# Block-sparse attention and a soft mixture of experts on one core: combine tiles of one width, own PSUM banks for the last pair, a new order of all steps

## The chip, the cores and the metric

The kernel runs on one core of a Trainium2 chip. Its time is the device time of one execution in microseconds (us); three executions of the kernel before took 200.78, 201.76 and 205.98 us, median 201.76 us. All names below are those of the profile: PE is the matmul engine (TensorE), PEld its weight loads, DVE the vector engine, ACT the scalar engine, POOL the GpSimd engine, SP the engine that issues nearly all DMAs.

## What is computed

Attention over 4 batches, 8 heads, 768 positions, 64 values a head; each query sees its own 96 last positions and 8 global keys, with a bias that falls with distance. Its output, 3072 tokens of 512 values, goes through a soft mixture of 8 experts with 4 slots each:

```
scores = q @ k.T / 8 + bias(distance, head), masked;  a = softmax(scores);  x = a @ v
logits = x @ phi                                # 3072 x 32
d = softmax(logits over tokens); slots = d.T @ x            # 32 x 512
h = relu(slots[e] @ w1[e]); slot_out[e] = h @ w2[e]         # 8 experts, 512 -> 1024 -> 512
c = softmax(logits over slots);  out = c @ slot_out         # 3072 x 512
```

## The kernel before

The program is written as named steps. A table, ORDER (line 53, 795 entries), names them in the order in which they are issued; each engine executes its own instructions in that order and waits by semaphores for the others. Nothing else decides the order.

**Attention.** A unit is one batch and one pair of heads, 16 units of two heads. For each: `scores` (L560, PE, three parts), `biased` (L569, DVE, adds the bias and keeps a maximum), `max_t` and `max_r` (L576, L581), `exponential` (L585, ACT), `w_hi` (L588, ACT, half precision) and its remainder `w_lo` (L595, on POOL, as `w_lo_dve` on DVE), `v_hi` and `v_lo` (L528 to L538, the same split of v; `v_hi_act` is ACT, `v_hi_dve` DVE), `values` (L612, PE), `ev_sums`, `ev_recs`, `ev_mul` (L625 to L637, DVE, the division), `tr` (L649, PE transposes; part 0 has 480 columns, part 1 has 288), `tr_copy` or `tr_copy_dve` (L654 ACT, L658 DVE, out of PSUM), and every second unit `logits` (L679). PSUM has eight banks: two for `xx` (the `values` output), two tiles `sc[0]`, `sc[1]` of two banks each for `scores`, and two small ones `m` in turn.

**Last pair.** After the last unit the four banks of `sc` become four banks `l`, handed out in turn by `left()`. In the kernel before, the logits of the last unit and its two transposes are put into `sc[0]` and `sc[1]` by a table, LAST_BANKS: both transposes are halves of one tile, `sc[1]`. Then come the softmax over tokens, `disp` (L762) and `slots` (L857).

**Experts.** `hid` (L879) and `proj` (L907) are the two matmuls of the experts; `late` reloads the places of the first weights with the second half of the second weights. `proj(0, ...)` gives output columns 0 to 255, `proj(1, ...)` columns 256 to 511; `osc`, `spread` and `sot` bring each half to four strips of 32 partitions.

**Combine.** `comb(n, b)` (L976), for half n and batch b, has seven matmuls, one for each tile of 120 tokens, the last of which has 48 tokens (TN is 120 six times and 48 once). Tile j = 2s + k reads the strip of 32 partitions number s, so the order k = 0: s = 0, 1, 2, 3 and k = 1: s = 0, 1, 2 puts four and three matmuls on different strips. Those with s < 3 write banks `l` (each bank takes two), the one with s = 3 writes a bank `m`. `outc` (L794 DVE, L797 ACT) copies each bank `l`, `outl` the bank `m` of two batches; `out` and `outl` DMAs (L988, L991) write 240 KB and 192 KB to memory. A matmul in 32-bit floats shows as two records in the trace.

**Other steps that the change moves.** `load_qk`, `load_v`, `extra`, `piece`, `free` and `late` are DMAs on SP's queue, in order; `chk_*` (L995 to L1019) compute a flag that says whether the fast path was valid; `cmax`, `csub`, `cexp`, `csum`, `crec`, `cmul` (L932 to L948) are the softmax over slots; `warm` (L549) is a matmul of a constant that is thrown away.

Of the kernel before, what the change touches and what calls it, by code (L numbers as in the profile page):

```python
# [10 lines left out]
F32 = mybir.dt.float32  # L11
# [10 lines left out]
B, H, S, D = 4, 8, 768, 64  # L22
DM = H * D
NG = 8
KB = 120
P = 128
# [19 lines left out]
OUT_PART = ((0, HF), (HF, HF))  # L46
# [266 lines left out]
def tile_attention_moe(ctx: ExitStack, tc: tile.TileContext, qk, v, phi, w1, w2, nn, out):  # L313
# [182 lines left out]
    nc.gpsimd.memset(eps[:, NJ - 1:NJ], 1.0e30)  # L496
    nc.gpsimd.memset(eps[0:TN[6], NJ - 1:NJ], RS_EPS)
    nc.scalar.activation(out=state[0:1, 4:5], in_=nc.const_aps.tensor(1.0, [1, 1], F32), func=AF.Exp)


    sc = [pss.tile([P, 2, 512], F32, name=f"sc{k}", tag=f"sc{k}") for k in range(2)]
    xx = psx.tile([P, 2, 512], F32, name="x", tag="x")
    mxs, nbs, rcs, ms = {}, {}, {}, {}

    def tb(u):
        return tbuf[u % 3]

    LAST_BANKS = {("logits", last): (0, 0), ("tr", last, 0): (1, 0), ("tr", last, 1): (1, 1)}

    def bank(key):  # L510
        if key in LAST_BANKS:
            k, i = LAST_BANKS[key]
            return sc[k][:, i]
        return psm.tile([P, 512], F32, name="m", tag="m")

    end = {}

    def left():

        if not end:  # L520
# [167 lines left out]
    def logits_all(u):  # L688
        b, p = units[u]
        if p != NP - 1:  # L690
            return
        lp = ms.pop(u)
        al = wk.tile([P, 6], F32, name="al", tag="al")
        als[b] = al
        for r, n in PARTS:
            nc.vector.tensor_tensor_reduce(out=lsb[r, 0:n], in0=lp[r, 0:n], in1=lsb[r, 0:n], scale=1.0, scalar=-3.0e38,  # L696
                                           op0=ALU.add, op1=ALU.max, accum_out=al[r, 4:5])
# [161 lines left out]
    def put(g):  # L859
        moe.put_slots(sl, mo.pop(("s", g))[:, 2 * NS * g:2 * NS * g + 2 * NS], 2 * g, 2 * g + 2)  # L860


    slv = Moe.slot_view(sl)
    parts = range(len(OUT_PART))
    hss = [xn01[:, WP:WP + DF], places[9][:, 0:DF]]
    hts = [[x.rearrange("p (c s m) -> p c s m", c=4, s=4) for x in y]
           for y in ((sacc, xn01[:, WP + DF:WP + DF + 512]), (places[10][:, 3 * DM:4 * DM], places[11][:, 3 * DM:4 * DM]))]
    osb = [places[8][:, at:at + w] for at, w in OUT_PART]
    sots = [places[8][:, DM + at:DM + at + w] for at, w in OUT_PART]
    obs = {k: places[10 + i // 3][:, DM * (i % 3):DM * (i % 3) + DM] for i, k in enumerate(OUT_SETS)}  # L870
    obl = [(places[8][:, DF:2 * DF], places[9][:, DF:2 * DF])[at // HF][:, B * (at % HF):B * (at % HF) + B * w].rearrange("p (b f) -> p b f", f=w) if at % HF + w <= HF
           else places[18][:, 0:B * w].rearrange("p (b f) -> p b f", f=w) for at, w in OUT_PART]

    def hid(a, c):
        if c == 0:
            mo["h", a] = [left(), left()]
        for n in range(2):
            for s in range(4):
                nc.tensor.matmul(out=mo["h", a][n][32 * s:32 * s + 32, :], lhsT=slv(a, c, s),  # L879
                                 rhs=wt[0, 4 * a + s, c // 2][:, (c % 2) * DF + 512 * n:(c % 2) * DF + 512 * n + 512],  # L880
                                 start=(c == 0), stop=(c == 3), skip_group_check=True)

    def relu(a, n):
        nc.scalar.activation(out=hss[a][:, 512 * n:512 * n + 512], in_=mo["h", a][n], func=AF.Relu)
# [70 lines left out]
    def by_slot(b):  # L955
        return lnat_all[:, 8 * b:8 * b + 8, :].rearrange("p t s -> p (t s)")[:, 0:2 * KB]
# [4 lines left out]
    def comb(n, b):  # L961
        w = OUT_PART[n][1]
        step = HF // w
        if w == P or b % 2 == 0:
            mo["l", n, b] = bank(("last", n, b))
        for s in range(3):
            mo["y", n, b, s] = left()
        for i in range(step):
            for k in range(2):
                for s in range(4):  # L970
                    j = 2 * s + k
                    if j == NJ:
                        continue
                    at = w * (2 * i + k) if s < 3 else w * ((b + i) % 2)
                    o = mo["y", n, b, s] if s < 3 else mo["l", n, b if w == P else b - b % 2]
                    nc.tensor.matmul(out=o[0:TN[j], at:at + w], lhsT=by_slot(b + i)[32 * s:32 * s + 32, KB * k:KB * k + TN[j]],  # L976
                                     rhs=sots[n][32 * s:32 * s + 32], start=True, stop=True)
# [117 lines left out]
def general(ctx, tc, moe, qk, v, phis, w1, w2, ngl, nlo, ident, out):  # L1095
# [113 lines left out]
    with ExitStack() as g3:  # L1209
        sb = g3.enter_context(tc.tile_pool(name="gsb3", bufs=1))  # L1210
        wp = g3.enter_context(tc.tile_pool(name="gwp", bufs=8))
        ps = g3.enter_context(tc.tile_pool(name="gps3", bufs=4, space=PSUM))
        cache = {}

        def weight(m, e, half):
            if (m, e, half) not in cache:
                t = wp.tile([P, 2048], F32, name="gw", tag="gw")
                nc.sync.dma_start(out=t, in_=(w1, w2)[m][e][:, 2048 * half:2048 * half + 2048])
                cache[(m, e, half)] = t
            return cache[(m, e, half)]  # L1220

        slv = Moe.slot_view(sl)
        hs = sb.tile([P, DF], F32, name="ghs")
        hts = [sb.tile([P, 8, P], F32, name=f"ght{a}") for a in range(2)]
        for a in range(2):
            moe.hidden(ps, slv, lambda e, half: weight(0, e, half), a, hs)
            moe.hidden_t(ps, hs, hts[a])
        moe.constants()
        st = sb.tile([P, NQ, 4], F32, name="gcs")
        ex = sb.tile([P, NQ, NS], F32, name="gex")  # L1230
        sps = [sb.tile([P, 8, P], F32, name=f"gsp{i}") for i in range(2)]
        ct = sb.tile([P, B * S], F32R, name="gct")
        moe.softmax(lnat, st, ex)
        for k in range(3):
            moe.split(ex[:, 8 * k:8 * k + 8], sps[k % 2])
            moe.weights_by_slot(ps, sps[k % 2], ct, [(t, P, P * (8 * k + t)) for t in range(8)])
        oh = sb.tile([P, DM], F32R, name="goh")
        sot = sb.tile([P, DM], F32R, name="gso")
        obs = [sb.tile([P, 4 * HF], F32, name=f"gob{i}") for i in range(2)]
        for n, (at, w) in enumerate(OUT_PART):  # L1240
            o = ps.tile([P, 512], F32, name="gop", tag="x")
            for a in range(2):
                moe.project(o, hts[a], lambda e, h: weight(1, e, h), n, a)
            moe.slots_out(o[:, 0:w], oh[:, at:at + w], sot[:, at:at + w])
            moe.combine(ps, ct, n, sot[:, at:at + w], obs, out)
# [61 lines left out]
```

## Time and profile before

| what | value |
|---|---|
| three executions | 200.78, 201.76, 205.98 us (median 201.76) |
| profiled execution, its own time | 200.85 us |
| its span, first to last instruction | 199.1 us |
| mean granted PE clock over the span | 0.96 of full speed |
| PE, DVE, ACT, POOL busy in the span | 91%, 74%, 63%, 48% |
| DMA, all queues | 61.40 MB, mean 308 GB/s |

The time of an execution is 1.75 us more than its span. A row of the page's first part gives an engine's busy time, its share of the span and its instructions; shares over the whole span are means of stages with different limits, so the rows further down are taken stage by stage. In a time line a row is one or several like instructions: the start and the time from first start to last end, both in us from the start of the span, engine, line, what is written and read, the number of records, and in brackets how long the engine had been idle and what ended that.

### The profile page before, as it was taken

How to read it: one execution, taken by the hardware profiler on the slowest of the kernel's cores; microseconds unless marked ns; L12 is line 12 of the kernel's file. 1: busy time of each engine (PE TensorE's matmuls, PEld its weight loads, DVE VectorE, ACT ScalarE, POOL GpSimd, SP SyncE). 2: the span in 40 equal slices, each digit the busy share in tenths (PEclk: the TensorE clock that was granted, in tenths of full speed). 3: DMA queues.
4: the chain of work that ended last, by engine and by line, in shares of the span. 5: the costliest groups of instructions: out<-in, count | busy, mean ns of one | idle time of the engine just before them, and what ended most of it. 6: DMA issues, size and time to landing. Idle time of an engine off the chain costs nothing.

```text
span 199.1 us, 6434 instructions
## 1 busy us (share of the span) xinstructions
PE 181.5 (91%) x2638; PEld 125.3 (63%) x2638; DVE 146.9 (74%) x390; ACT 125.9 (63%) x162; POOL 94.9 (48%) x137
## 2 busy tenths in 40 slices
PE   8989899999989999999999978979999999999930
PEld 2657689978878888887898766634334544435400
DVE  5999999999999998999999999885007402435130
ACT  3499899999979899999999995320003123333210
POOL 6816886878885885797679536002002400000000
PEclk9999999999999999999999999999999999998555
DMA  6999999999998969764579998999999963858672
GB/s 212 421 380 402 403 403 358 412 408 353 360 408 285 407 196 371 230 199 161 172 216 318 334 346 329 396 322 430 398 393 389 388 244 103 245 155 266 207 235 82
DMA packets 15937, 61.40 MB, mean 308 GB/s; under 512 B 1786, under 2 KB 2938, under 8 KB 14106
## 3 DMA queue, kind: packets, MB, share of 16 engines
q1 hardware_dynamic: 15896, 60.89, 84.2%
q8 instruction: 23, 0.38, 0.7%
q14 instruction: 16, 0.13, 0.2%
q10 hardware_dynamic: 2, 0.00, 0.0%
HBM read 54.59 MB, written 6.29 MB: 306 GB/s over the span
## 4 chain that ended last, share of the span: by engine, by line
PE 56%; DVE 19%; DMA 13%; issue 6%; ACT 2%; DVEq 0%; ACTq 0%
PE x L612 10%; PE sc L560 9%; PE x L907 8%; PE l L879 7%; DMA raw<-in_qk_dram 7%; PE l L976 7%; DMA wp<-in_v_dram 6%; DVE tb L569 4%; DVE xn L637 4%; PE m L649 3%; PE m L976 3%; DVE v L538 2%; PE m L679 2%; PE m L762 2%; DVE ph L595 2%
## 5 line engine op out<-in xcount | busy, mean ns | idle before, releaser
L595 POOL TENSOR_TENSOR ph<-tb,ph 128x432 f16<-128x432 f32 x77 | 80.3, 1072 | 30.9 <-ACT ph L588 25.5
L585 ACT ACTIVATE tb<-tb,nb 128x1296 f32<-128x1296 f32 x32 | 43.6, 1375 | 1.7 <-DVE nb L581 1.7
L612 PEld LDWEIGHTS <-ph 128*128 128x128 f16 x1248 | 41.4, 97 | 5.1 <-issue 3.8
L612 PE MATMUL x<-v,ph 128*128 128x65 f16 (+1 forms) x1248 | 43.1, 193 | 1.5 <-DVE ph L595 0.6
L588 ACT CAST ph<-tb 128x1296 f16<-128x1296 f32 x31 | 39.5, 1273 | 2.8 <-PE x L612 1.7
L560 PE MATMUL sc<-raw 64*128 64x216 f32 (+1 forms) x392 | 39.3, 338 | 1.5 <-DVE mx L569 1.1
L560 PEld LDWEIGHTS sc<-raw 64*128 64x128 f32 x392 | 32.3, 186 | 6.4 <-issue 3.0
L637 DVE CUSTOM_DVE_ANT_1 xn<-x,rc 120x448 f32<-120x448 f32 x32 | 18.9, 620 | 0.4
L569 DVE CUSTOM_DVE_ANT_1 tb<-sc,tt,mx 128x864 f32<-128x864 f32 x16 | 17.8, 1114 | 1.0 <-DVE mx L569 0.5
L649 PE MATMUL m<-ident,xn 120*128 120x120 f32 x105 | 15.8, 276 | 0.7 <-DVE al L696 0.3
L976 PE MATMUL l<-wp,lnat 32*120 32x256 f32 x96 | 15.2, 484 | 0.9 <-DVE flag L1026 0.4
L538 DVE SCALAR_TENSOR_TENSOR v<-vt,v 128x896 f16<-128x896 f32 x14 | 15.2, 1085 | 0.1
L649 PEld LDWEIGHTS m<-ident,xn 120*128 120x128 f32 x105 | 10.7, 140 | 4.2 <-issue 1.1
L595 DVE TENSOR_TENSOR ph<-tb,ph 128x432 f16<-128x432 f32 x19 | 13.3, 720 | 0.0
L976 PEld LDWEIGHTS l<-wp,lnat 32*120 32x120 f32 x96 | 7.2, 203 | 8.3 <-issue 5.2
L879 PE MATMUL l<-wp,sl 128*32 128x512 f32 x80 | 10.7, 593 | 0.0
L797 ACT COPY sacc<-m 128x128 f32<-128x128 f32 x1 | 0.3, 265 | 15.2 <-PE m L892 15.2
L794 DVE COPY raw<-l 120x512 f32<-120x512 f32 x2 | 1.4, 692 | 11.3 <-PE l L976 11.3
L531 ACT ACTIVATE v<-vt 128x896 f16<-128x896 f32 x10 | 9.5, 950 | 0.0
L887 DVE TENSOR_SCALAR xn<-l 128x512 f32<-128x512 f32 x2 | 1.3, 686 | 11.0 <-PE l L879 11.0
L569 DVE CUSTOM_DVE_ANT_1 tb<-sc,xtt,mx 128x864 f32<-128x864 f32 x8 | 8.9, 1114 | 0.7 <-PE sc L560 0.4
L948 POOL TENSOR_TENSOR lnat<-lnat,cst 120x256 f32<-120x256 f32 x4 | 2.5, 629 | 13.9 <-DVE cst L945 13.5
(229 smaller groups left out, 299.6 us busy)
## 6 DMA issues: line engine op xcount, KB each, us to landing
raw<-in_qk_dram SPq DMA_DIRECT2D x14, 832.0 KB, 5.6
wp<-in_w_dram SPq DMA_DIRECT2D x10, 1024.0 KB, 8.7
wp<-in_w_dram SPq DMA_DIRECT2D x16, 512.0 KB, 7.7
vt<-in_v_dram SPq DMA_DIRECT2D x14, 448.0 KB, 5.0
tb<-in_w_dram SPq DMA_DIRECT2D x3, 1024.0 KB, 7.3
out_dram<-tb SPq DMA_DIRECT2D x9, 240.0 KB, 3.2
wp<-in_qk_dram SPq DMA_DIRECT2D x2, 832.0 KB, 9.4
raw<-in_w_dram SPq DMA_DIRECT2D x2, 832.0 KB, 4.6
```

The costliest lines, as they stand in the source:

```text
L538: nc.vector.scalar_tensor_tensor(out=vlo[k].rearrange("p j i d -> p (j i) d"), in0=vraws(u).rearrange("p j i d -> p (j i) d"), scalar=V_SC ...
L560: nc.tensor.matmul(out=z[:, i, at:at + n], lhsT=r_[r, KCOL[j]:KCOL[j] + KR], rhs=r_[r, KW + KB * j:KW + KB * j + n], start=True, stop=True)
L569: nc.vector.tensor_tensor_reduce(out=tb(u)[:, :, BW * k:BW * k + BW], in0=sc[(3 * u + k) % 2][:, :, 0:BW], in1=table.unit(u % NP, k), scal ...
L585: nc.scalar.activation(out=t, in_=t, func=AF.Exp, bias=nbs[u], scale=T_SC)
L588: nc.scalar.copy(out=blocks(phi_[i])[:, :, 0:QW], in_=tb(u)[:, i].rearrange("p (s c) -> p s c", c=QW))
L595: (engine or nc.gpsimd).tensor_tensor(out=blocks(plo_[i])[:, c, 0:QW], in0=tb(u)[:, i].rearrange("p (s c) -> p s c", c=QW)[:, c], in1=bloc ...
L612: nc.tensor.matmul(out=x[:, (D + 1) * t:(D + 1) * t + d], lhsT=w[:, c:c + P], rhs=vv[:, j, i, 0:d], start=(z == 0), stop=(z == len(ops) - ...
L637: nc.vector.tensor_tensor_reduce(out=xnb[(u // 2) % 3][:, :, c:c + D], in0=xv[:, i, :, 0:D], in1=rcs.pop((u, i)).unsqueeze(2).to_broadcast ...
L649: nc.tensor.transpose(out=m[:, at:at + KB], in_=xnb[(u // 2) % 3][:, t, P * (p % 2):P * (p % 2) + P], identity=ident[0:KB, 0:KB])
L879: nc.tensor.matmul(out=mo["h", a][n][32 * s:32 * s + 32, :], lhsT=slv(a, c, s), rhs=wt[0, 4 * a + s, c // 2][:, (c % 2) * DF + 512 * n:(c ...
L907: nc.tensor.matmul(out=xx[32 * s:32 * s + 32, n % 2, 0:w], lhsT=hts[a][c // 4][:, c % 4, s], rhs=wt[1, 4 * a + s, half][:, c0 + w * c:c0 + ...
L976: nc.tensor.matmul(out=o[0:TN[j], at:at + w], lhsT=by_slot(b + i)[32 * s:32 * s + 32, KB * k:KB * k + TN[j]], rhs=sots[n][32 * s:32 * s + ...
```

## The change

`comb` gives every matmul a stationary operand and an output of 120 columns (KB) in place of TN[j], so that the last tile, 48 before, has 120 as well; the 72 output rows more are not read. LAST_BANKS becomes a list of three keys that take their bank from `left()`: the two transposes and the logits of the last unit have a bank each, and the tokens' transposes after them take the fourth and then the first again. The small tile `al` has four buffers instead of two. One place in `obl` and a `cache.clear()` are in code that this configuration does not run. ORDER is new, with 798 entries.

```diff
-ORDER = [('load_qk', 0), ('load_v', 0), ('load_qk', 1), ('load_v', 1), ('load_v', 3),
+ORDER = [('load_qk', 0), ('load_qk', 1), ('load_v', 0), ('extra', 2), ('load_v', 1),
...
-    LAST_BANKS = {("logits", last): (0, 0), ("tr", last, 0): (1, 0), ("tr", last, 1): (1, 1)}
+    LAST_BANKS = (("logits", last), ("tr", last, 0), ("tr", last, 1))
 
     def bank(key):
         if key in LAST_BANKS:
-            k, i = LAST_BANKS[key]
-            return sc[k][:, i]
+            return left()
         return psm.tile([P, 512], F32, name="m", tag="m")
...
-        al = wk.tile([P, 6], F32, name="al", tag="al")
+        al = wk.tile([P, 6], F32, name="al", tag="al", bufs=4)
...
-                    nc.tensor.matmul(out=o[0:TN[j], at:at + w], lhsT=by_slot(b + i)[32 * s:32 * s + 32, KB * k:KB * k + TN[j]],
+                    nc.tensor.matmul(out=o[0:KB, at:at + w], lhsT=by_slot(b + i)[32 * s:32 * s + 32, KB * k:KB * k + KB],
                                      rhs=sots[n][32 * s:32 * s + 32], start=True, stop=True)
...
```

What ORDER moves, counted from the two tables: of the steps that may run on either of two engines, `v_hi` of unit 6 goes from POOL to ACT and that of unit 7 from DVE to ACT; five `tr_copy_dve` of the units before the last are four of part 0 and one of part 1 before, and one and four now; of `w_lo` the same number is on DVE, at other units. Eight more `warm` matmuls stand among the first units. `chk_l(0)`, `cmax(0)` and `cmax(1)` come earlier, `chk_l(1)` after the last `values`. The combine keeps its place among the `proj` steps.

Three places show what stands in each engine's queue. ACT and DVE at the last copies of the outputs, before (bank `l_3016` is the first of the last batch; `m_2999` the narrow one):

```order
L797 COPY tb0_95<-l_3000 120x512 [waits DMAHW6_49,PE_49]
L797 COPY tb0_95<-l_3002 120x512 [waits PE_49]
L797 COPY wp9_92<-m_2999 48x512 [waits PE_49]
L794 COPY v16_100<-l_3018 120x512 [waits DMAHW2_49,PE_49]
L794 COPY v16_100<-l_3017 120x512 [waits DMAHW5_49]
L794 COPY v16_100<-l_3016 120x512
```

and now:

```order
L796 COPY tb0_95<-l_3011 120x512 [waits PE_49]
L796 COPY wp9_92<-m_3008 48x512 [waits PE_49]
L796 COPY v16_100<-l_3027 120x512 [waits DMAHW6_49,DMAHW2_49,PE_49]
L796 COPY v16_100<-l_3026 120x512
L793 COPY v16_100<-l_3028 120x512 [waits DMAHW2_49,PE_49]
```

Three copies in a row on DVE have become one on DVE and two on ACT. PE and ACT at the last pair, before (the transposes, the logits of unit 14 from `tt`, those of unit 15 from `xta`; then ACT's copy of the second transpose):

```order
L649 MATMUL sc1_176<-ident_78,xn01_106 128x120 [waits DVE_49]
L649 MATMUL sc1_176<-ident_78,xn01_106 128x120 x6
L679 MATMUL sc0_175<-tt_102,phis_80 32x240 [waits DVE_49]
L679 MATMUL sc0_175<-xta_103,phis_80 32x240 [waits DVE_49]
L679 MATMUL sc0_175<-xta_103,phis_80 32x240 [waits Activation_49]
L654 COPY xta_103<-sc1_176 128x288 [waits DVE_49]
```

and now:

```order
L648 MATMUL l_2507<-ident_78,xn01_106 128x120 [waits DVE_49]
L648 MATMUL l_2515<-ident_78,xn01_106 128x120 x3
L678 MATMUL l_2521<-tt_102,phis_80 32x240 [waits Activation_49]
L678 MATMUL l_2521<-xta_103,phis_80 32x240 [waits DVE_49]
L678 MATMUL l_2521<-xta_103,phis_80 32x240 [waits Activation_49]
L653 COPY xta_103<-l_2515 128x288 [waits PE_49]
```

ACT's copy waited for DVE and now waits for PE. SP at the start of the program, before (`raw0`, `raw1`, `wp9`, `wp8` take the queries and keys of units 0 to 3, then `raw1` and `raw0` those of units 5 and 4):

```order
L424 DMA wp9_92<-in_qk_dram 128x1664
L413 DMA xtt_104<-in_w2_dram 128x416
L424 DMA wp8_91<-in_qk_dram 128x1664 [waits DMAHW0_49]
L427 DMA wp7_90<-in_v_dram 128x896 [waits DMAHW1_49]
L413 DMA ph1_99<-in_w2_dram 128x512 [waits DMAHW7_49]
L424 DMA raw1_94<-in_qk_dram 128x1664 [waits DMAHW0_49,PE_49]
L424 DMA raw0_93<-in_qk_dram 128x1664 [waits DMAHW1_49]
```

and now:

```order
L424 DMA wp9_92<-in_qk_dram 128x1664
L424 DMA raw0_93<-in_qk_dram 128x1664 [waits DMAHW1_49,DMAHW0_49,PE_49]
L427 DMA wp7_90<-in_v_dram 128x896
L424 DMA wp8_91<-in_qk_dram 128x1664 [waits DMAHW2_49]
L413 DMA raw0_93<-in_w1_dram 128x384 [waits DMAHW3_49]
L424 DMA raw1_94<-in_qk_dram 128x1664 [waits DMAHW5_49,PE_49]
```

Unit 4's queries and keys are issued ahead of unit 3's, and wait for PE to be done with unit 0's scores.

## Rows read from the trace of the kernel before

**Rows 1.** The page: each engine's busy us, share of the span, instructions.

```profile
PE 181.5 (91%) x2638; PEld 125.3 (63%) x2638; DVE 146.9 (74%) x390; ACT 125.9 (63%) x162; POOL 94.9 (48%) x137
```

**Rows 2.** Stretches: length, busy us of PE, PEld, DVE, ACT, POOL, clock, DMA share, GB/s.

```profile
10.00:60.00 50.00, 46.76 (x792) 39.74 (x791) 48.88 (x121) 46.61 (x48) 36.26 (x36) 1.00 1.01 388
60.00:110.00 50.00, 49.85 (x922) 42.47 (x919) 48.23 (x124) 47.95 (x56) 38.46 (x38) 1.00 0.75 256
110.00:125.40 15.40, 13.26 (x276) 10.62 (x273) 15.19 (x41) 11.95 (x18) 7.75 (x9) 1.00 0.95 339
...
164.00:175.00 11.00, 11.00 (x142) 5.01 (x138) 3.45 (x9) 3.22 (x6) 0.00 (x0) 1.00 0.59 178
175.00:183.00 8.00, 7.36 (x52) 3.47 (x48) 3.31 (x7) 2.47 (x5) 0.00 (x0) 1.00 0.67 188
183.00:191.00 8.00, 7.73 (x27) 3.30 (x26) 1.66 (x3) 2.37 (x5) 0.00 (x0) 0.50 0.77 244
```

**Rows 3.** Time line of PE: one combine of the first half.

```profile
163.96 0.70 PE L976 MATMUL l<-wp,lnat 32*120 32x256 f32 x6
164.59 0.63 PE L976 MATMUL m<-wp,lnat 32*48 32x256 f32 x2
165.15 0.70 PE L976 MATMUL l<-wp,lnat 32*120 32x256 f32 x6
165.78 1.07 PE L907 MATMUL x<-wp,xn 128*32 128x256 f32 x16
```

**Rows 4.** Time line of PE: the first half's fourth combine; then the second half's.

```profile
175.01 0.70 PE L976 MATMUL l<-wp,lnat 32*120 32x256 f32 x6
...
179.24 1.12 PE L976 MATMUL l<-wp,lnat 32*120 32x256 f32 x8
180.60 0.84 PE L976 MATMUL l<-wp,lnat 32*120 32x256 f32 x4 [0.24 <-ACT tb L797]
```

**Rows 5.** Time lines of ACT and DVE: copies of the second half's combines.

```profile
179.96 0.58 ACT L797 COPY tb<-l 120x512 f32<-120x512 f32 x1 [2.41 <-PE l L976]
182.65 1.07 ACT L797 COPY vt<-l 120x512 f32<-120x512 f32 x2 [2.10 <-PE l L976]
186.83 1.07 ACT L797 COPY tb<-l 120x512 f32<-120x512 f32 x2 [3.10 <-PE l L976]
...
191.03 1.89 DVE L794 COPY v<-l 120x512 f32<-120x512 f32 x3 [3.47 <-PE l L976]
```

**Rows 6.** Line 976: weight loads, ns min/median/max; then three of them in time.

```profile
L976 PEld LDWEIGHTS l<-wp,lnat x96: 174/178/320, 164.0 to 189.9; 32*120 32x120 f32 x96
...
L976 PEld LDWEIGHTS m<-wp,lnat x16: 114/118/189, 164.6 to 188.8; 32*48 32x48 f32 x16
...
163.96 0.29 PEld L976 LDWEIGHTS l<-wp,lnat 32*120 32x120 f32 x6 [0.41 <-issue]
```

**Rows 7.** Output DMAs: issue to landing; two stretches in which they are alone.

```profile
DMA to landing us min/median/max: 2.4/3.1/4.9
...
168.00:170.00 2.00, 2.00 (x29) 0.97 (x28) 0.69 (x1) 1.07 (x2) 0.00 (x0) 1.00 0.89 309
194.00:195.00 1.00, 0.00 (x0) 0.00 (x0) 0.00 (x0) 0.00 (x0) 0.00 (x0) 0.50 0.92 295
```

**Rows 8.** Time lines of DVE, ACT and PE: the last pair.

```profile
128.10 0.66 DVE L658 COPY xta<-sc 128x480 f32<-128x480 f32 x1 [0.19 <-PE sc L649]
...
130.01 0.40 DVE L696 CUSTOM_DVE_ANT_0 lsb<-sc,lsb 96x240 f32<-96x240 f32 x1 [0.92 <-PE sc L679]
...
128.79 0.40 ACT L654 COPY xta<-sc 128x288 f32<-128x288 f32 x1 [1.05 <-DVE xta L658]
...
136.50 1.92 PE L879 MATMUL l<-wp,sl 128*32 128x512 f32 x16
```

**Rows 9.** Groups of ACT and waits of PE: a split of v; a late load.

```profile
L531 ACT ACTIVATE v<-vt 128x896 f16<-128x896 f32 x10 | 9.5, 950 | 0.0
...
PE sc L560 <- DMA raw<-in_qk_dram: 0.4, 1, 0.4
```

More of the change, by code (lines that the diff above doesn't have):

```diff
@@ L871, in tile_attention_moe @@
     obl = [(places[8][:, DF:2 * DF], places[9][:, DF:2 * DF])[at // HF][:, B * (at % HF):B * (at % HF) + B * w].rearrange("p (b f) -> p b f", f=w) if at % HF + w <= HF
-           else places[18][:, 0:B * w].rearrange("p (b f) -> p b f", f=w) for at, w in OUT_PART]
+           else places[9][:, 0:B * w].rearrange("p (b f) -> p b f", f=w) for at, w in OUT_PART]
     def hid(a, c):
@@ L1240, in general @@
         for n, (at, w) in enumerate(OUT_PART):
+            cache.clear()
             o = ps.tile([P, 512], F32, name="gop", tag="x")
```

2 lines of the change are left out of this document (1 added, 1 removed).

## The prediction

> **What bounds the kernel now.** The page's busy times come first [rows 1]: PE is busy 91% of the span, DVE 74%. These are means, so the stretches are read next [rows 2]. In the attention, 10 to 125.4 us, PE and DVE share the bound: DVE idles 1.12 us in the first 50, 1.77 in the next 50 and 0.21 in the last 15.4, PE 3.24, 0.15 and 2.14. From 164 to 175 us, where combines alternate with projections, PE is busy 11.00 of 11.00 us. From 183 us the granted clock is 0.50, the lower of the two levels (1.2 GHz), and the last combines run at it. In the 8.00 us before that PE had been busy 7.36 at the full clock, the upper level.
>
> The time lines say what a combine costs. In the first half [rows 3] three matmuls on strips 0, 1, 2 (six records) start at 163.96, the narrow one at 164.59, three more at 165.15, the projection at 165.78: 0.63 + 0.56 + 0.63 = 1.82 us. The six records of three matmuls take about as long as the two records of the narrow one alone. So strips overlap, except for the 48-column matmul, which runs by itself between the two groups.
>
> **The combine's width.** With 120 columns the narrow matmul is like the three ahead of it, and on a strip of its own, so I expect it to run beside them, and the second group to follow without a break. What a second round on occupied strips adds is in [rows 3, 4]: eight records (a group of three and the next combine's first) take 1.12 us where six take 0.70, so 0.42. A combine should then take 0.63 + 0.42 = 1.05 us, 0.77 less. No row has four strips of 120 columns at once, so the other bound is no gain; the nearest row, three strips, speaks for the upper value, and I take it.
>
> The wider weights could take some of it back: a load of 120 columns takes 178 ns, one of 48 columns 118 [rows 6], 0.06 us more for each of 16 loads, 1.0 us if nothing hid it. But six loads are done in 0.29 us, not in 6 x 0.178 = 1.07, so they run side by side and I cost the width at nothing; the loads of the other strips hide it, and without them the 1.0 us would be back. The Trainium skill ("TensorE: Matmul & The Clock Gate", LDWEIGHTS) has the load take columns / 1.2 ns whatever the rows, an estimate of 60 ns for 72 columns more; by that alone the sum would lose 1.0 us, and the trace agrees with the size of a load and not with its standing alone.
>
> **First half:** three of its combines lie between projections on a PE without idle time: 3 x 0.77 = 2.3 us. **The fourth, and the first of the second half,** give 1.54, of which I take 1.45, because the DVE copy that follows the spread now waits for DVE instead of PE.
>
> **Second half.** Nothing is left between its combines, and each waits for a bank. ACT's copies start at 179.96, 182.65, 186.83 and DVE's last at 191.03 [rows 5]: one period of 2.69 us at full clock, then 4.18 and 4.20 at half clock. From a copy's start to the next matmul is 0.64 us (179.96 to 180.60); that wait stays and becomes the larger part. After it the two matmuls left take 0.84 [rows 4], the wide fourth goes with them, and the second round adds 0.42: 0.64 + 0.84 + 0.42 = 1.90 us. Three periods go from 11.07 to 5.7 us: 2.4 us saved by the width and 3.0 by being done about when the clock fell. The last three copies, 1.89 us on DVE alone, are now one on DVE and two on ACT, which takes 1.07 for two; ACT has the narrow tile's copy ahead of them, 0.5 us or so, so I take 0.5. **Sum on PE and copies: 2.3 + 1.45 + 5.4 + 0.5 = 9.6 us.**
>
> **What is late next: the output DMAs.** From the fourth combine on, 15 DMAs of 240 KB and two of 192 KB have to be written, 4.08 MB. Stretches with outputs alone move 309 GB/s at a share of 0.89 and 295 at 0.92 [rows 7], so 320 to 350 at a full queue; I take 320: 12.75 us. Call S the start of the fourth combine, 175.0 before [rows 4]. The first of these DMAs can go out a combine and a copy after S, 1.05 + 1.89 / 3 = 1.7 us; the last byte is moved at S + 14.4 and lands some 1.6 us later (the fastest DMA lands in 2.4 us, of which 0.8 is its transfer): S + 16.0. Before, the last copy ended at 192.92 and its DMA landed 3.1 us later, S + 21.0. So this path saves 5.0 us behind S and 2.3 ahead of it, 7.3 us. It ends later than the copies' path, which would save 9.6, and so it binds. Since the queue will not be full at every moment I take **7.0 us**, with 6 and 9.6 as ends.
>
> **Last pair.** ACT's copy of the second transpose had been idle 1.05 us waiting for DVE's copy of the first, which read the other half of the same tile; it ran at 128.79 [rows 8]. With own banks it can start when PE has transposed, at about the 128.10 at which DVE started, 0.69 us earlier, and DVE's copy need not wait for the second transpose (0.19). The last logits wait for both copies, and DVE idled 0.92 us for them before 130.01. I take 0.5 us, between 0 and 0.9; the token softmax that follows passes it on whole.
>
> **The new order of the attention.** Unit for unit it is nearly the same list. ACT takes two splits of v, 0.95 each [rows 9], and three copies of 480 columns in place of 288; by DVE's 0.66 against ACT's 0.40 [rows 8] that is under 0.3 each: 2.7 us more on ACT, which idles 8.9 us in 10 to 125.4 [rows 2]. DVE gives off one split and three times the same difference. Each of the eight constant matmuls is priced as one record of a combine, 0.42 / 2 = 0.21 us, together 1.7, beside PE's 3.24 us of idle time in the first stretch; without that cover they would cost their 1.7. On SP's queue unit 4's queries go ahead of units 2's values and 3's queries and must wait there for unit 0's scores; unit 4's load is the only one PE waited for, 0.4 us [rows 9]. Behind it now stand two loads that are needed a unit earlier. The bounds: DVE's idle time, 3.1 us, is the most that can be won; all of ACT's 2.7 and PE's 1.7 the most I can name as lost. I take 0, near the middle.
>
> **Sum:** against the profiled execution, 200.85 us (span 199.1 and 1.75 around it; 0.9 below the median of 201.76): 200.85 - 7.0 - 0.5 = **193.3 us**.
>
> **Rivals.**
>
> *A, the outputs do not bind.* If outputs move at 350 GB/s or more, or the loads' end leaves the queue freer, the copies' path rules: 200.85 - 9.6 - 0.5 = 190.7. For it: the share stayed below 1 in both stretches. Chance 0.15.
>
> *B, the fourth strip does not overlap.* Then 0.77 x 8 is not won, the clock falls where it did, and only the last copies and the last pair remain: 199.9 us. For it: no row shows four. Against it: the narrow matmul differs from its neighbours in nothing but width, strip and bank. The Trainium skill ("TensorEngine Tiling", Key Properties) has a change of tiling mode drain the engine; by it the width alone kept the fourth apart, which no row can tell from strip or bank. Chance 0.12.
>
> *C, the new order costs the attention what it gains behind.* With DVE idle 3.1 us in 115 there is no room for a wait in the wrong place; 0.3 us a unit is 4.8 us, time 198. Against it: the list of each unit and the distance of loads from their use hardly change. Chance 0.08.
>
> *D, slower: the clock falls early.* In this trace it fell in a stretch with PE 92% busy, while in 164 to 175, fully busy, it stood. If the shorter combines let it fall at the first of them, six projections (1.07 us each [rows 3]) and eight combines (four of 1.05, four with 1.26 of PE work) are doubled: 15.7 us, of which the output queue's lag hides 2.3: 206.7 us. Break-even with 201.76 is a fall with about 11 us of PE work left, shortly ahead of the third combine; a fall in the second half is hidden or costs up to 3 us. Against it: PE stays without idle time there. Chance 0.03.
>
> **How the numbers follow.** Forecast 0.62 (190.5 to 196, from its own ends), A 0.15, B 0.12, C 0.08, D 0.03. The range 189.5 to 198 takes in forecast, A and most of C; it leaves out B, D and the tails. A measurement of this kernel tells about 2% from no change. Faster than 197.7: forecast and A, and half of C and a little of B, 0.83; within 2%: the rest of B and C, 0.13; slower: D and a bit for an order that fails, 0.04.
>
> **What would show it.** Right: in the time line a combine has eight and then six records of 120 columns without a group of its own for the narrow one, and 1.0 to 1.1 us to the next projection; copies of the second half come every 1.9 to 2.1 us; output DMAs late in it land in more than 4 us, with a share above 0.9; ACT's copy at the last pair no longer ends a wait on DVE; `hid` starts within 2 us of 136 (136.50 now [rows 8]). Wrong: the fourth's records again stand apart; `hid` starts after 139; the clock line falls before the last five slices.

## The result, and the profile after

The changed kernel takes 194.51 us (median of 4, 193.40 to 197.23), the kernel before 202.16 in the same session: ratio 0.9626, interval 0.9518 to 0.9733. Timed again later, the ratio was 0.9639 (0.9567 to 0.9711). Medians include executions that were disturbed by a lower clock; the ratios leave these out. The forecast was 193.3 us. The profiled execution took 193.68 us, with a span of 191.9.

The page's busy times (engine, busy us, share of the span, instructions; [rows 1]) and three stretches of the end (columns as in [rows 2]):

```profile
PE 171.1 (89%) x2645; PEld 123.0 (64%) x2645; DVE 139.9 (73%) x385; ACT 128.7 (67%) x167; POOL 92.4 (48%) x137
...
161.00:172.00 11.00, 11.00 (x160) 5.96 (x158) 3.54 (x9) 4.99 (x10) 0.00 (x0) 1.00 0.66 203
172.00:180.00 8.00, 5.84 (x58) 3.91 (x56) 4.45 (x9) 4.77 (x10) 0.00 (x0) 1.00 0.83 234
180.00:188.00 8.00, 0.00 (x0) 0.00 (x0) 0.00 (x0) 0.02 (x1) 0.00 (x0) 0.57 0.91 279
```

PE is busy 10.4 us less, with seven constant matmuls more (20 for 13: eight more among the first units, one fewer at the last pair). From 180 us no engine computes, and the queue still works at a share of 0.91. The clock fell at 181.1 us, 2.2 us after PE's last matmul, where it costs nothing.

The time line of PE, one combine, answers [rows 3]:

```profile
160.94 0.48 PE L975 MATMUL l<-wp,lnat 32*120 32x256 f32 x3
160.96 0.47 PE L975 MATMUL m<-wp,lnat 32*120 32x256 f32 x1
161.26 0.39 PE L975 MATMUL l<-wp,lnat 32*120 32x256 f32 x3
161.28 0.37 PE L975 MATMUL m<-wp,lnat 32*120 32x256 f32 x1
161.47 0.60 PE L975 MATMUL l<-wp,lnat 32*120 32x256 f32 x6
...
163.01 0.48 PE L975 MATMUL l<-wp,lnat 32*120 32x256 f32 x3
```

The records of `m` now lie among those of `l`; from the combine's start to the projection (162.00) it is 1.06 us, 1.82 before, 1.05 forecast. The copies of the second half (time lines of ACT and of DVE) answer [rows 5]:

```profile
175.20 1.07 ACT L796 COPY vt<-l 120x512 f32<-120x512 f32 x2 [0.96 <-PE l L975]
...
176.95 1.07 ACT L796 COPY tb<-l 120x512 f32<-120x512 f32 x2 [0.21 <-PE l L975]
...
178.96 1.06 ACT L796 COPY v<-l 120x512 f32<-120x512 f32 x2
```

They come 1.75 and 2.0 us apart (2.69, 4.18 and 4.20 before; 1.90 forecast), and the last one ends at 180.02, 9.8 us behind the fourth combine's start; my sum had 10.6. The last pair (time lines of DVE, ACT and PE) answers [rows 8]:

```profile
125.90 0.66 DVE L657 COPY xta<-l 128x480 f32<-128x480 f32 x1 [0.34 <-PE l L648]
...
126.20 0.40 ACT L653 COPY xta<-l 128x288 f32<-128x288 f32 x1
...
133.69 0.64 PE L878 MATMUL l<-wp,sl 128*32 128x512 f32 x4
```

ACT's copy no longer waits for DVE's. `hid` starts at 133.69, 2.81 us earlier and 0.3 us outside the 2 us around 136 that I had named. The output DMAs (times from issue to landing, answering [rows 7]; then SP's issues in time):

```profile
DMA to landing us min/median/max: 2.5/4.2/4.8
...
174.31 2.26 SPq L987 DMA_DIRECT2D out_dram<-tb  x3
178.33 1.75 SPq L987 DMA_DIRECT2D out_dram<-vt  x3
180.18 2.21 SPq L987 DMA_DIRECT2D out_dram<-tb  x3
182.49 0.95 SPq L990 DMA_DIRECT2D out_dram<-wp  x1
183.53 2.59 SPq L987 DMA_DIRECT2D out_dram<-v  x3
```

The last copy is done at 180.02 and its DMA goes out at 185.29; before, it went out 0.03 us behind the copy. It lands at 189.63. So the outputs bind, as forecast, but 19.4 us behind the fourth combine's start and not 16.0. The queue's share in the four slices of 2 us from 174 us is 0.87, 0.96, 0.71 and 0.81, not above 0.9 throughout as I had expected. The hole from 176.58 to 178.33 is SP reading the flag that decides on the general code.

The table gives what the profiles of all runs show, in us: where the last unit's values start, where `hid` starts, from the first combine to the fourth, from the fourth to the end of the span, and (where it went out singly) to the last output's landing. The clock came to its upper level at 3.5 to 5.9 us, but at 9.8 us in the profile of "late flag" and at 9.9 in that of "half rows", of which only the tail is used.

| kernel | values(15) | `hid` | comb 1 to 4 | comb 4 to end | to landing |
|---|---|---|---|---|---|
| before | 122.86 | 136.50 | 11.05 | 24.05 | 21.7 |
| changed | 120.95 | 133.69 | 9.27 | 21.67 | 19.4 |
| changed, again | 123.62 | 136.36 | 9.27 | 21.60 | 19.6 |
| width alone | 123.71 | 137.36 | 8.78 | 21.35 | 19.5 |
| width undone | 122.05 | 134.78 | 11.54 | 23.92 | 22.1 |
| banks alone | 123.85 | 136.81 | 11.05 | 25.31 | 23.1 |
| order alone | 121.99 | 137.02 | 11.55 | 25.51 | 23.7 |
| 64 columns | 123.20 | 135.94 | 11.59 | 24.89 | 23.1 |
| 96 columns | 123.30 | 136.04 | 9.28 | 21.55 | 19.6 |
| half rows | | | 9.28 | 19.87 | |
| late flag | 125.16 | 137.90 | 9.27 | 21.08 | 18.6 |
| late flag, fourth early | 123.19 | 135.93 | 7.54 | 22.65 | 20.2 |
| late flag, joined | 121.69 | 134.43 | 9.27 | 22.06 | 20.2 |
| late flag, joined, half rows | 123.75 | 136.48 | 9.27 | 18.43 | 14.7 |

### The profile page after: what moved, and what is told of

Read it like the earlier page. It is cut to its first block, busy times and chain, and to the rows that moved or that the text cites. A ratio compares the mean times of both kernels' runs of the same rounds, so it can differ in the third digit from the quotient of the medians.

```text
span 191.9 us, 6448 instructions
## 1 busy us (share of the span) xinstructions
PE 171.1 (89%) x2645; PEld 123.0 (64%) x2645; DVE 139.9 (73%) x385; ACT 128.7 (67%) x167; POOL 92.4 (48%) x137
## 4 chain that ended last, share of the span: by engine, by line
PE 59%; DVE 12%; ACT 11%; POOL 7%; issue 5%; DVEq 0%; ACTq 0%; POOLq 0%
PE x L611 12%; PE sc L559 11%; PE x L906 8%; PE l L878 7%; POOL ph L594 5%; DVE tb L568 5%; PE l L975 4%; ACT tb L584 4%; PE m L648 4%; ACT ph L587 3%; PE m L678 2%; PE m L761 2%; DVE xn L636 1%; DVE v L537 1%; PE l L761 1%
## 5 line engine op out<-in xcount | busy, mean ns | idle before, releaser
L594 POOL TENSOR_TENSOR ph<-tb,ph 128x432 f16<-128x432 f32 x77 | 78.3, 1045 | 31.7 <-ACT ph L587 29.0
L594 DVE TENSOR_TENSOR ph<-tb,ph 128x432 f16<-128x432 f32 x19 | 11.9, 643 | 0.1
L530 ACT ACTIVATE v<-vt 128x896 f16<-128x896 f32 x12 | 11.4, 949 | 0.0
L975 PE MATMUL l<-wp,lnat 32*120 32x256 f32 x96 | 10.3, 400 | 1.0 <-ACT tb L796 0.5
L975 PEld LDWEIGHTS l<-wp,lnat 32*120 32x120 f32 x96 | 6.6, 177 | 4.4 <-issue 1.6
L568 DVE CUSTOM_DVE_ANT_1 tb<-sc,xta,mx 128x864 f32<-128x864 f32 x8 | 8.9, 1114 | 0.2 <-POOL ph L594 0.2
L568 DVE CUSTOM_DVE_ANT_1 tb<-sc,tt 128x864 f32<-128x864 f32 x8 | 8.4, 1052 | 0.2 <-PE sc L559 0.2
L883 ACT ACTIVATE xn<-l 128x512 f32<-128x512 f32 x1 | 0.6, 597 | 10.9 <-PE l L878 10.9
```

Of the source, the lines that this page charges most:

```text
L568: nc.vector.tensor_tensor_reduce(out=tb(u)[:, :, BW * k:BW * k + BW], in0=sc[(3 * u + k) % 2][:, :, 0:BW], in1=table.unit(u % NP, k), scal ...
L594: (engine or nc.gpsimd).tensor_tensor(out=blocks(plo_[i])[:, c, 0:QW], in0=tb(u)[:, i].rearrange("p (s c) -> p s c", c=QW)[:, c], in1=bloc ...
L975: nc.tensor.matmul(out=o[0:KB, at:at + w], lhsT=by_slot(b + i)[32 * s:32 * s + 32, KB * k:KB * k + KB], rhs=sots[n][32 * s:32 * s + 32], s ...
```

## Experiments

**Width alone.** The kernel before with

```diff
-matmul(out=o[0:TN[j], at:at + w], lhsT=...[32 * s:32 * s + 32, KB * k:KB * k + TN[j]],
+matmul(out=o[0:KB, at:at + w], lhsT=...[32 * s:32 * s + 32, KB * k:KB * k + KB],
```

> The kernel before with one edit: the combine's narrow matmul takes 120 columns. Order, banks and copies stay. Theory 1 (width does the tail, the output DMAs then bind): PE as in the changed kernel, 1.06 us from a combine to the next projection; three combines ahead of the fourth give 3 x 0.76 = 2.3 us; behind the start of the fourth the end comes 21.7 us later as in the changed kernel, 24.1 before: 2.4 us. Together 4.7 us, about 196.2 us against 200.85. Theory 2 (my forecast's sizes: 2.3 + 5.0): 193.5 us. Rival (the fourth strip runs beside the others only because of the new order or banks): combines stay at 1.82 us and the time stays at 200.9. hid starts at 136.5 by all.

196.46 us (median of 6), ratio 0.9675 (0.9606 to 0.9743). The narrow matmul runs among its neighbours (time line of PE):

```profile
164.83 0.48 PE L976 MATMUL l<-wp,lnat 32*120 32x256 f32 x3
164.85 0.47 PE L976 MATMUL m<-wp,lnat 32*120 32x256 f32 x1
```

Three combines give 11.05 - 8.78 = 2.27 us as forecast, and from the fourth to the end it takes 21.35, 2.7 us less than before. So by the trace theory 1 holds, and the forecast's 5.0 us behind the fourth combine does not. The time alone could not tell: the ratio is 6.6 us of 202.6 (5.2 to 8.0), between the 4.7 of theory 1 and the 7.3 of theory 2. One line carries most of the change.

**Width undone.** The changed kernel with that edit reversed.

> The changed kernel with the narrow matmul back at 48 columns; new order and new banks stay. Theory 1: hid starts at 133.7 as in the changed kernel (2.8 us earlier than before), combines are back at 1.82 us, the clock falls in the second half again, the last copies on two engines give up to 0.8 us: 200.85 - 2.8 - 0.5 = 197.5 us. Theory 2 (forecast's sizes: order 0, last pair 0.5, last copies 0.5): 199.9 us. Rival (order and banks gave nothing, all of it is width): 200.9 us and hid at 136.5.

200.13 us (6), ratio 0.9885 (0.9825 to 0.9944): 2.3 us of 202.6 (1.1 to 3.5), between the 0.95 of theory 2 and the 3.35 of theory 1. The narrow matmul stands apart again, in the new order and beside the new banks (time line of PE):

```profile
162.04 0.70 PE L975 MATMUL l<-wp,lnat 32*120 32x256 f32 x6
162.67 0.63 PE L975 MATMUL m<-wp,lnat 32*48 32x256 f32 x2
163.23 0.70 PE L975 MATMUL l<-wp,lnat 32*120 32x256 f32 x6
```

So strip and bank, which are the same in the changed kernel, do not keep it apart. Of the 2.8 us in front of `hid` 1.7 are there in this execution.

**Banks alone.** The kernel before with

```diff
-            k, i = LAST_BANKS[key]
-            return sc[k][:, i]
+            return left()
...
-        al = wk.tile([P, 6], F32, name="al", tag="al")
+        al = wk.tile([P, 6], F32, name="al", tag="al", bufs=4)
```

> The kernel before with one edit: the last pair's two transposes and its logits get banks of their own (and the small tile al four buffers). Theory 1 (the last pair gave 0.9 us in the changed kernel, 0.65 up to the last logits and 0.26 behind): hid starts at 135.6 instead of 136.5, time 200.0 us. Theory 2 (forecast): 0.5 us, hid at 136.0, 200.3 us. Rival (the new order is needed for it): hid at 136.5. The tail as before.

202.19 us (12), ratio 0.9943 (0.9898 to 0.9988). ACT's copy waits for PE, 0.36 us, in place of 1.05 for DVE:

```profile
129.09 0.40 ACT L653 COPY xta<-l 128x288 f32<-128x288 f32 x1 [0.36 <-PE l L648]
```

From the last pair's first three transposes (those of unit 14) to `hid` it takes 10.61 us, 11.29 before: 0.68. With the new order too it is 10.38 in the changed kernel and 10.37 with the width undone: 0.9. The time alone shows no more than a small gain.

**Order alone.** The changed kernel with both of those edits put back.

> The changed kernel with both the 48 columns and the shared banks put back: the new order of all steps alone. Theory 1 (the order itself gains in the attention): the last pair's transposes start at 124.7 (126.6 before), hid at 134.6, last copies on two engines 0.5: 200.85 - 1.9 - 0.5 = 198.4 us. Theory 2 (forecast, the order is worth 0 in the attention): hid at 136.5 and 200.3 us. Rival (the earlier transposes came from the banks): transposes at 126.6.

202.56 us (12), ratio 0.9967 (0.9919 to 1.0016). The values of the last unit start early, at 121.99, but `hid` at 137.02, which neither theory had. Stretches of this kernel around the token softmax (columns as in [rows 2]) show why:

```profile
128.90:131.00 2.10, 0.22 (x3) 0.13 (x2) 1.71 (x11) 0.77 (x3) 0.00 (x0) 1.00 0.98 409
132.00:133.00 1.00, 1.00 (x14) 0.35 (x6) 0.78 (x5) 0.15 (x2) 0.00 (x0) 0.55 1.04 410
133.00:135.00 2.00, 2.00 (x19) 1.02 (x16) 1.23 (x5) 0.00 (x0) 0.63 (x1) 0.50 1.05 421
135.00:136.00 1.00, 1.00 (x13) 0.34 (x6) 0.14 (x1) 0.00 (x0) 0.00 (x0) 0.74 1.04 424
```

PE idles 1.88 us, and the granted clock falls to the lower level, 1.2 GHz, at 132.1 for 3.4 us; the last dispatch's two parts take 1.70 and 1.78 us in place of 1.06. With the banks PE idles 1.54 us there and the clock stood. From the same transposes to `hid` it takes 12.66 us with the order alone, 10.61 with the banks alone, 10.4 with both. In the ten profiles that have both, PE idles 1.54 to 1.55 us there and the clock never falls; of the order alone there is one profile, so that this order needs the banks is likely and not shown.

**64 and 96 columns** for the last strip's matmul, in the changed kernel:

```diff
+    FW = [KB] * (NJ - 1) + [64]
...
-matmul(out=o[0:KB, at:at + w], lhsT=...[32 * s:32 * s + 32, KB * k:KB * k + KB],
+matmul(out=o[0:FW[j], at:at + w], lhsT=...[32 * s:32 * s + 32, KB * k:KB * k + FW[j]],
```

> The changed kernel with the combine's last matmul 64 columns wide instead of 120 (48 are needed). Theory 1 (a matmul runs beside its neighbours when it takes the same part of the array's columns, and 64 or fewer take half): it stands apart as with 48 columns, combine 1.8 us from its first matmul to the next projection, copies of the second half 2.7 us apart. Rival 1 (only the very same width runs beside): the same 1.8 us here, and the run with 96 columns tells. Rival 2 (any width above 48 will do): 1.06 us.

> The changed kernel with the combine's last matmul 96 columns wide instead of 120. Theory 1 (above 64 columns it takes the whole width as its neighbours with 120 do): it runs beside them, combine 1.06 us, time as the changed kernel, 193.7 us. Rival 1 (only the very same width runs beside): combine 1.8 us and about 197.5 us by the order and banks alone.

201.56 and 195.91 us, one run each. Time lines of PE, with 64 columns:

```profile
163.19 0.70 PE L977 MATMUL l<-wp,lnat 32*120 32x256 f32 x6
163.82 0.64 PE L977 MATMUL m<-wp,lnat 32*64 32x256 f32 x2
164.40 0.70 PE L977 MATMUL l<-wp,lnat 32*120 32x256 f32 x6
```

and with 96:

```profile
163.29 0.49 PE L977 MATMUL l<-wp,lnat 32*120 32x256 f32 x3
163.31 0.45 PE L977 MATMUL m<-wp,lnat 32*96 32x256 f32 x1
```

64 columns stand apart (1.84 us a combine), 96 run beside 120 (1.07). It is not equal width that counts, but which side of a step between 64 and 96 the width lies on. The Trainium skill ("TensorEngine Tiling (Array Packing)", Key Properties) has a change of tiling mode drain the engine; the four widths agree with that, if 48 and 64 columns are one mode and 96 and 120 another. That it is a drain no run shows.

**Half rows.** The changed kernel, output DMAs of half the size:

```diff
-dma_start(out=out_block(out, n, b, s), in_=obs[n, b, s][0:KB])
+dma_start(out=out_block(out, n, b, s)[0:60], in_=obs[n, b, s][0:60])
```

> The changed kernel; every output DMA writes only the first half of its rows (60 of 120, 24 of 48), as many DMAs with half the bytes; the other half of the output is left out. Theory 1 (the output bytes bind behind the copies): the copies still end about 180.0 us into the span, the last DMA goes out within 0.6 us of that and lands some 2.5 us later, 2.2 us before the end: span 185.3, time about 187.1 us, 6.6 less than 193.7. Rival 1 (the number of DMAs or SP's issuing binds): the last DMA still goes out at 185.3 and the time stays within 1 us of 193.7. Rival 2 (something behind the copies on another engine sets the end): also 193.7.

193.49 us (5), ratio 0.9604 (0.9521 to 0.9686): not told apart from the changed kernel's 0.9639. Theory 1 falls. The last copy ended at 184.36 and its DMA went out at 188.15. SP's issues in time, then the queues from 181.8 to 183.4 us, inside the first row:

```profile
181.45 2.40 SPq L987 DMA_DIRECT2D out_dram<-vt  x3
183.94 2.69 SPq L987 DMA_DIRECT2D out_dram<-tb  x3
...
q1 hardware_dynamic: 72, 0.12, 23.1%
q8 instruction: 1, 0.02, 4.2%
```

The three issues of `vt` took 0.37, 1.49 and 0.36 us, those of `tb` 1.78, 0.36 and 0.37; the data queue was 23% busy around the 1.49 and 41% from 183.9 to 185.8 us, around the 1.78. SP's issuing, 7.9 us from 181.45 for ten DMAs, is as long as in the changed kernel, 7.8 from 178.33. From the fourth combine to the end it takes 19.87 us, 1.7 less than in the changed kernel, where theory 1 wanted 6.6.

**The changed kernel again**, in one session with the next two.

> The changed kernel once more, beside the two runs that follow. By all theories 193.4 to 195.3 us, ratio 0.963 to the kernel before; the DMA of the last output lands 19.4 us after the start of the fourth combine.

195.92 us (6), ratio 0.9639. The tail is the same to 0.1 us; `hid` came at 136.36. The wait (us, times, longest), a time line of PE and two stretches:

```profile
PE sc L559 <- DMA raw<-in_qk_dram: 1.7, 1, 1.7
...
51.90 1.44 PE L559 MATMUL sc<-raw 64*128 64x216 f32 x8 [1.74 <-DMA raw<-in_qk_dram]
...
50.00:52.00 2.00, 0.26 (x6) 0.16 (x5) 1.98 (x5) 2.00 (x3) 1.62 (x3) 1.00 0.99 415
52.40:55.70 3.30, 3.30 (x35) 1.77 (x32) 1.57 (x5) 1.76 (x2) 1.39 (x2) 0.50 1.04 426
```

PE waits for queries and keys out of a queue at a share of 0.99, and behind that the clock is at the lower level for 3.4 us. The first profile had 0.91 us of idle time at this place and no fall. Of eight more profiles of the new order, half rows left out, seven name a wait of PE on such a load of 1.5 to 1.8 us, the eighth one of 1.84 that it puts down to DVE, and three show a fall at about 52 us. The three profiles of the old order show waits of 0.4 to 1.0 us on such loads and no fall in the attention.

**Late flag.** `chk_sum` behind the last combine, `set_flag` behind the last copy, so that SP reads the flag last.

```diff
-..., ('outl', 0), ('chk_sum', 0), ('outc_dve', 0, 3, 2), ..., ('out', 1, 0, 1), ('set_flag', 0), ...
+..., ('comb', 1, 3), ('chk_sum', 0), ..., ('out', 1, 3, 0), ('set_flag', 0)]
```

> The changed kernel with the flag that decides whether the general code is needed computed and read last: its two steps stand behind the last combine and the last copy, so SP reads it behind its last output DMA and not between the fourth and the fifth combine's. Theory 1 (while SP reads the flag, 1.75 us, the output queue runs partly empty: a share of 0.71 and 0.81 in the two slices behind it, 0.96 us of 4): the last output lands 1.0 us earlier, at most 1.75, time 0.5 per cent less than the changed kernel's. Rival (the queue holds enough work to cover the read): the same time within 0.3 us. Rival 2 (the read at the end, 1.3 us on five engines, comes to lie on the path): not faster, since it ends long before the last output lands.

195.51 us (6), ratio 0.9685 (0.9630 to 0.9740). In the trace the last landing comes 18.6 us behind the fourth combine, 1.0 earlier, as theory 1 had it; of that 0.5 to 0.6 reach the end of the span. The times show no gain (0.9639 in the same session), since the head varies by more.

**Late flag, fourth combine early.**

```diff
 ('proj', 1, 1, 1),
+('outc_act', 0, 2, 2), ('outc_dve', 0, 2, 1), ('outc_act', 0, 2, 0), ..., ('comb', 0, 3),
 ('proj', 1, 1, 2), ..., ('proj', 1, 1, 3),
-('comb', 0, 3),
```

> The run with the late flag, and the first half's fourth combine two projections earlier: one projection and not three between the third and the fourth, its copies shared by ACT and DVE. Theory 1 (the outputs bind from the first combine on: 6.3 MB from 162.7, at 300 GB/s 21 us, landing at 185.3 if the queue never ran empty, 189.6 in the changed kernel): the fourth combine's outputs go out 2 us earlier and fill the stretch from 170 to 172 us, last landing 1.0 to 1.5 us before that with the late flag alone, about 191.5 us. Rival (the second half's copies, which end at 180.0 either way, and what they leave in the queue set the end): the same time as with the late flag alone.

195.05 us (6), ratio 0.9662 (0.9603 to 0.9722). From the first combine to the last landing it takes 27.7 us, 27.9 with the late flag alone: the rival holds. The fourth combine's outputs left 1.5 us earlier, counted from the first combine, and the queue ran low again (a share of 0.25 from 177 to 178 us) before the fifth's came.

**Late flag, joined DMAs.** One DMA of 720 KB a combine:

```diff
-dma_start(out=out_block(out, n, b, s), in_=obs[n, b, s][0:KB])
+dma_start(out=...[OUT_BLOCK * i:OUT_BLOCK * (i + 3)].rearrange("(s p x) -> p s x", s=3, p=KB),
+          in_=places[10 + i // 3][0:KB, 0:3 * DM].rearrange("p (s x) -> p s x", s=3))
```

> The run with the late flag, and the three output DMAs of a combine joined in one of 720 KB (eight DMAs in place of 24, the same bytes); it goes out when the third copy is done, up to 1 us later than the first did. Theory 1 (SP's issuing binds the end: with half the bytes the last DMA still went out 3.8 us behind the last copy, 5.3 in the changed kernel, and SP's issues of 0.7 to 1.9 us add up to that): the last DMA goes out within 0.6 us of the last copy, the last output lands 24.5 to 26.5 us after the start of the first combine, against 27.9 with the late flag and 28.7 in the changed kernel; 1.4 to 3 us less than the late flag's run, from an equal start of the combines. Theory 2 (the bytes bind after all, 4.08 MB at 300 GB/s from the fourth combine on): the last DMA goes out early, but lands at the same 27.9 us, or up to 1 us later since it starts later.

196.08 us (6), ratio 0.9665 (0.9597 to 0.9733). The last DMA went out at 181.37, 0.6 us behind the last copy, and landed at 191.19, 29.5 us behind the first combine. That is theory 2 in kind, but 1.6 us worse than the late flag alone where theory 2 allowed 1.0. SP's last issue, then the stretches (share and GB/s last):

```profile
181.37 2.01 SPq L988 DMA_DIRECT2D out_dram<-v  x1
...
181.00:183.00 2.00, 0.00 (x0) 0.00 (x0) 0.00 (x0) 0.00 (x0) 0.00 (x0) 1.00 1.01 353
183.00:185.00 2.00, 0.00 (x0) 0.00 (x0) 0.00 (x0) 0.00 (x0) 0.00 (x0) 0.60 0.99 301
...
187.00:189.00 2.00, 0.00 (x0) 0.00 (x0) 0.00 (x0) 0.00 (x0) 0.00 (x0) 0.50 0.50 175
189.00:191.00 2.00, 0.00 (x0) 0.00 (x0) 0.00 (x0) 0.00 (x0) 0.00 (x0) 0.50 0.20 73
```

Now the queue is full to 187 us, and then fewer and fewer of the 16 DMA engines have work: 16 packets are under way at 186.0 us, 8 at 188.25 and one at 190.25.

**Late flag, joined DMAs, half rows.** Both edits together.

> The run with joined DMAs, and each of them writes only the first half of its rows (60 of 120, 24 of 48); the other half of the output is left out. Half the bytes alone and a third of the DMAs alone moved the end by under 2 us. Theory 1 (two limits of about the same length lie behind the copies, SP's issuing and the bytes in the queue; either alone hides the other): with both eased the end follows the copies: the last DMA goes out within 0.6 us of the last copy, which ends 19.1 us after the first combine's start, lands 2.5 to 4 us later, and the span ends 24 to 26 us after that start, against 30.9 in the changed kernel: 5 to 7 us less. Rival (something else behind the copies, the landing itself or the end of the program, sets the time): 29 us or more, as in the runs with either alone.

191.74 us (4), ratio 0.9493 (0.9431 to 0.9555), 1.5% or 2.9 us below the changed kernel. Time lines of ACT and SP:

```profile
181.76 1.06 ACT L796 COPY v<-l 120x512 f32<-120x512 f32 x2
...
182.84 0.77 SPq L988 DMA_DIRECT2D out_dram<-v  x1
```

The last DMA went out 0.03 us behind the last copy and the last output landed 14.7 us behind the fourth combine, 4.9 earlier than in the changed kernel; the late flag, which half rows alone did not have, has 1.0 of this. Either limit alone had hidden the other. The landing took 4.9 us where theory 1 had 2.5 to 4. The span ends 18.4 us behind the fourth combine, 3.2 earlier, and 27.7 behind the first, outside the 24 to 26 of theory 1, since something else comes last: PE's branch over the general code, which can start only once the late flag is read, took 6.0 us and ended at 189.84, 2.1 us behind the last landing.

## Why the prediction was right, and where it was not

- **The combine's width: right in mechanism and size.** 1.06 us for 1.05, and 2.27 us for 2.3 in the first half. Rival B is out: the width was what kept the fourth strip apart. The wider loads cost nothing that the combine shows. What the prediction says of the size of a load holds for the difference alone, 178 - 118 = 60 ns; the loads themselves are longer than the rule that it quotes.
- **The second half on PE and the copies: right.** 5.3 us for three periods against 5.7, and the last copies on two engines. The later periods, 1.75 and 2.01 us, lie about the 1.9 to 2.1 that I had named.
- **The outputs bind: right place, mis-sized.** I had the last landing at S + 16.0 from the bytes at 320 GB/s, and 21.0 before; it was 19.4 to 19.6, and 21.7 before (I had given the last DMA the median of 3.1 us to land; it took 3.7). So that step saved 3.2 us behind the fourth combine (means of the table: 24.74 in five kernels with narrow, 21.54 in four with wide matmuls), not 5.0. The 3.2 is a mean: with narrow matmuls the end depends on when the clock falls. It fell 8.0 and 8.3 us behind S in the kernel before and with the width undone, and the end came 24.05 and 23.92 behind S, 2.3 to 2.7 us later than with wide matmuls; it fell 4.4 to 6.8 us behind S in the other three, with 24.89 to 25.51. The step that failed is "the last byte is moved at S + 14.4", which takes the queue as full: the queue is fed by one engine that needs 0.4 to 0.5 us from an issue to the next at best, up to 1.95 for one at worst, and is away 1.75 us for a flag in between. Half the bytes alone give 1.7 us of the tail, a third as many DMAs alone nothing; both together, with the late flag, bring the landing 4.9 us forward. With the first half it makes 5.5 us, forecast 7.0.
- **The last pair: 0.9, forecast 0.5**, at the upper end; 0.7 of it by the banks alone.
- **The new order: 0 forecast, and 0 within its spread.** The first profile has 1.9 us, from which I concluded in the first expectations that the order gains. Ten profiles of the new order, half rows left out, start the last unit's values at 120.95 to 125.16, median 123.2; three of the old at 122.86 to 123.85. A gain of 0.5 us cannot be read from that. The zero may be a sum of two: the four profiles with a fall of the clock at about 52 us start them at 123.20 to 123.75, and five without one at 120.95 to 123.19, median 121.99 (the sixth, late flag, started with the late clock). So the order may gain and lose about 1.5 us; no run separates the two. What I had named as a price, two loads that stand behind unit 4's, is seen: waits of 1.5 us and more for queries and keys.
- **Sum.** 3.2 + 2.27 + 0.9 + 0.2 (from `hid` to the first combine) - 0.49 (from the first combine to the fourth the new order takes longer, 11.54 for 11.05 with narrow matmuls) = 6.1 us, and 6.6 with the 0.5 that the head's medians differ by. The last two terms are moved work: the description of the change has the combine keep its place among the projections, but the third now stands behind `proj(1, 1, 0)`, and the transposes of `turn` for the last batch, 0.35 us, now lie between the second combine and the third and not ahead of the first. The ratios are worth 7.6 and 7.3 us (0.9626 of 202.16, 0.9639 of 202.41; 5.4 to 9.7 and 5.8 to 8.8), the forecast was 7.5: the measured total does not tell the 6.1 from the 7.5. In the first pair of profiles the spans differ by 7.2 us: 1.9 in the head, 0.9 + 0.2, 1.8 to the fourth combine and 2.4 behind it. That the first profile's 193.68 comes so near to 193.3 is in part luck, since the head's 1.9 us, forecast 0, made up for what the outputs lacked.
- **The other rivals.** A: the outputs do bind. With both limits eased the time falls by 2.9 us, near the 2.6 between A's 190.7 and my 193.3, but there PE's branch ended the span, so the nearness says little. C: the order costs no 4.8 us, though its waits are real. D: with wide matmuls the clock did not fall in the combines; it fell in two other places, in the attention and, in one profile of the order alone, ahead of `hid`, behind pauses of PE of 1.65 to 1.88 us.

## To carry to other kernels

Small matmuls that are to run beside each other on strips of the array should have widths on the same side of the step, even if the extra columns are thrown away. Where a faster engine leaves the end to the output queue, count the issues and what else the issuing engine does, not only the bytes, and ease both before judging either. A difference between two single profiles is worth no more than the spread of the same term over several executions of one kernel.

## What the runs showed of the hardware

- SP's issue of an output DMA took 0.33 us when nothing held it, and up to 1.95. The long ones need no full queue (23% busy above). Of 23 issues of over 1.1 us in all runs with single output DMAs, 20 overlap a 16 KB fetch of instructions in the trace's DMA records, as the `q8` row shows for one; of the 236 issues under 0.45 us in the same runs 15 do. The Trainium skill ("Runtime: NRT & Kernel Launch", Instruction fetch mechanics) calls the cost of such a fetch mostly hidden; here it goes with 0.8 to 1.6 us of lost issuing. That the one causes the other was not tried.
- PE's branch over the code that is not run took 4.4 us in the changed kernel, 5.6 with the late flag and 6.0 to 7.7 with joined DMAs. The same page and section of the Trainium skill has a taken branch outside the fetched pages wait for a fetch; the trace agrees in direction, and no run shows what the length depends on.
- In front of the two falls of the clock to 1.2 GHz that are shown PE had idled 1.74 and 1.88 us; at the same two places it idled 0.91 and 1.54 us in the first profile, and the clock stood. With 64 columns it fell at 51.9 us behind a wait of 1.65. It stood behind a wait of 1.69 at 51.83 with the order alone and behind one of 1.78 at 45.35 in the run with the early fourth combine, so the idle time alone does not decide it.
